# Query parts ahead of v in the first loads, half-width costs in the plan, and new orders, in a fused attention and MoE kernel

## The chip, the cores and the metric

The kernel runs on one core of a Trainium2 chip. The metric is the device time in microseconds (us) of one execution. A profiled execution gives one timeline for each engine: TensorE (PE, with its weight loads as PEld), VectorE (DVE), ScalarE (ACT), GpSimd (POOL), SyncE (SP) and the DMA queues.

## The reference

There are 8 batches of 8 heads, with 576 tokens of 64 values in q, k and v, and 32 packed queries p for each head. The attention has two steps: p attends to k and v, which gives 32 packed rows per head, and q attends to these packed rows. The result, 4608 tokens by 512, goes through two matrices with a smooth ReLU between them.

```python
p_packed = sm_attn(p, k, v)
out = sm_attn(q, p_packed, p_packed)
# x: out as 4608 tokens by 512
h = x @ w_in                       # 512 by 2048
g = np.where(h >= 1, h, np.where(h <= -1, 0, (h + 1) ** 2 / 4))
return g @ w_out                   # 2048 by 512
```

`sm_attn` is a softmax of the scores, scaled by 1/8, times the values. Outputs are float32.

## The kernel before, in words

**The work of one batch.** `attention(b, key)` loads k, q and v of a batch as bfloat16 with 96 partitions. PE transposes k (`by_array`, line 423, tiles `tp` to `kT`), forms the scores of p against k (`scores`, `sp`, line 459), ACT takes the exponential (`ex`), and PE multiplies by v (`packed`, `pk`, line 479, the row sums in line 485). Three small copies and an add give `ppT`, the packed rows. From batch 3 on, and for one part of batch 2, the transposes of q and k are made by DMA.

Instead of making the attention's output and then multiplying by w_in, the kernel multiplies the packed rows by w_in (`mk`, tiles `mp`, then cast to `M`, lines 649 to 668). The weights of the second softmax, `A`, are made in transposed form: scores `s`, exponential `eT`, sums over heads' rows `sm`, reciprocal as a logarithm `ln` and an exponential `rc`, and the product `A`. For batches from 1 on this is `weights`; for batch 0 it is `first_weights` (line 570), which treats the tokens in two halves, x = 0 and x = 1, and the heads in two groups, g = 0 and 1.

A hidden tile (`hidden_tile`, line 717) is one of 16 blocks of 128 hidden columns for a batch: four matmuls of `M` with `A` give `h` (line 733), and three operations apply the smooth ReLU: ACT evicts `h` to `x` (line 738), DVE or ACT does a second step (line 743 or 745), and DVE writes `hT` (line 748). An output tile (`out_tile`, line 778) is 128 tokens: 16 matmuls of `hT` with `w_out`, one for each hidden block fi = 0 to 15 in order, called an o step here (line 795). The tiles are counted for pairs of batches, nine for each pair; the first four of the first pair are cut in two by `CUTS`, with their first parts of 4, 4, 8 and 8 steps kept and added later.

**The order of the work.** `Plan` (line 60) is a list scheduler that runs while the program is built. Each task has an engine (or two to choose from), a cost from the table `C`, a key and its dependences. The plan follows a clock for each engine and takes the task that can start first; among those that start within `wait` times the best one's cost, the lowest key goes first. The order in which the plan takes tasks is the order of the instructions on each engine, and engines work their queues in that order. `slack` and `margin` are extra lags for PE behind the other engines. Where PE would wait at the start, the plan puts in dummy matmuls on zeros (line 870). `KEYS` holds keys for the tasks of each batch's attention, in the order of `FIRSTS` for batch 0 and `UNITS` for the others. A hidden tile's key is its batch plus fi/16, an output tile's is 100 or more, `p4` is the key of the transposes of p for batches 2 to 7, and `bk` less 1 that of the evictions of the first pair's output tiles.

**The loads.** All big loads are issued from POOL's queue, in one order: `FIRST` (line 38), then `ORDER` (line 23). `k0`, `k1`, `v0`, `v1` are the halves of batch 0's k and v by heads; `q00` and `q01` are the x = 0 tokens of q for the two groups of heads, `r` the x = 1 tokens. `i0` to `i4` are column blocks of w_in (256, 256, 512, 512 and 512 columns), `o0` to `o3` four parts of w_out, with four hidden blocks each; `k0`, `q1` and so on in `ORDER` belong to batch 1, and `p` is the rest of p. `IDENT` says before which of the first loads POOL makes the identity that the transposes use. `FLOW` and `C` hold the times that the plan gives each load.

**Splits.** `SPLIT` names blocks of `M` whose cast is made for each group of heads by itself; `HALVED` names the hidden tiles of batch 0 that are made for each half of the tokens; `MERGED` names the halves x for which `ln` and `rc` of batch 0 are made for both groups in one operation.

Of the kernel before, what the change touches and what calls it, by code (L numbers as in the profile page):

```python
# [11 lines left out]
C = dict(load=2.93, half=1.45, w_in=2.55, w_out=2.55, rest=1.25, out=3.2, p=4.3, land=1.13, xt=6.5, xland=9.0,  # L12
         tpp=0.06, tp=0.0425, sc=0.0295, pk=1.0, s2=0.245, sm=0.245, M=0.216, h=0.49, o=0.2158, switch=0.11,
         Tca=1.12, Tcd=0.75, ex=0.807, ppo=0.4, ppT=0.41, ppa=0.4, ppd=0.22, rs=0.165,
         eT=0.741, ln=0.651, rc=0.683, A=0.816, Mca=1.014, Mcd=1.223, x=0.651, ta=0.681, td=0.459, hT=0.757, oba=0.586, obd=0.69, hx=2.181,
         array=0.2, tell=0.04, lead=0.12, until=18.0, feed=0.2374, margin=0.3641, slack=0.1788, wake=1.2, warm=7.0, early=0.2216, wait=0.002722, p4=999.0, bk=115.3)
OVER = {"ACT": 0.104, "DVE": 0.083}
NW, NO, NX, NB = 3, 2, 5, 6
DW, FILL = 256, 512
CUTS = (4, 4, 8, 8)  # L20
PARTS = len(CUTS)

ORDER = 'r i0 i1 i4 o0 i2 q0 i3 k1 k0 o1 v q1 o2 o3 p'

FIRSTS = "kT0 kT1 sc0 sc1 pk0 pk1 q00 q01 q10 q11 s200 s201 s210 s211 sm00 sm01 sm10 sm11 M0 M1 M2 M3 M4".split()
UNITS = "kT0 kT1 qT0 qT1 sc0 sc1 pk0 pk1 s20 s21 sm0 sm1 M0 M1 M2 M3".split()
KEYS = [
# [8 lines left out]
SPLIT = ((0, 0), (0, 1), (0, 2))  # L36
LATE = ()
FIRST = "k0 k1 v0 v1 q00 q01"
IDENT = 3
FLOW = {"k0": 1.48, "k1": 1.52, "v0": 1.5, "v1": 1.46, "q00": 0.8, "q01": 0.8, "r": 1.6, "in0": 2.25, "in1": 1.33}  # L40
BLOCKS = {0: (0, 256, 512, 1024, 1536, 2048)}
HALVED = (0, 1, 2)
MERGED = (0, 1)

TURNED = 3
BY_DMA = {2: "q1"}
# [13 lines left out]
class Plan:  # L60
# [154 lines left out]
def kernel(  # L215
# [10 lines left out]
    nc = tc.nc  # L226
# [9 lines left out]
    P = 128  # L236
# [10 lines left out]
    X = 2  # L247
# [20 lines left out]
    PE, ACT, DVE, DMA, SP = "PE", "ACT", "DVE", "DMA", "SP"  # L268
    add = plan.add
# [33 lines left out]
    hT = hid.tile([P, KF, 2 * S], bf16)  # L303
# [109 lines left out]
    def attention(b, key):  # L413
# [6 lines left out]
        A = lambda: get(b, "A", lambda: att.tile([P, G, X, HALF], bf16, tag="A", name="A"))  # L420
# [149 lines left out]
        def first_weights(deps, r):  # L570
            tq, eTs, As = {}, {}, {}
            eT = lambda g: get(b, "eT" + str(g), lambda: att.tile([P, X, HALF], bf16, tag="eT", name="eT"))
# [35 lines left out]
            for x in range(X):  # L608
                boxes, own, cps = [{}, {}, {}], None, []
                for g in range(G):  # L610
                    t = add(PE, C["tp"] * 6, key["q%d%d" % (x, g)], [part_of["q", x, g]] + ([own] if g else []),
                            lambda x=x, g=g, bx=boxes[0]: turn(x, g, bx), takes=None if g else "W", readers=0 if g else 2, mode=1)
                    own = own or t
                    cps.append(both(lambda eng, x=x, g=g, bx=boxes[0]: copy(qT()[:, x, g * w:(g + 1) * w], bx["tp"][:, g, :w])(eng),
                                    C["Tca"] * 0.55, C["Tcd"] * 0.55, key["q%d%d" % (x, g)], [t], frees=own))
                    tq[x, g] = t
                own = None
                for g in range(G):
                    ky = key["s2%d%d" % (x, g)]
                    t = add(PE, C["s2"] / 2, ky, deps[g] + [cps[g]] + ([own] if g else []),  # L620
                            lambda x=x, g=g, bx=boxes[1]: inner(x, g, bx), takes=None if g else "W", readers=0 if g else 2, mode=2)
                    own = own or t
                    K.setdefault((b, "s2"), []).append(t)
                    eTs[x, g] = add(ACT, C["eT"] * 0.6, ky, [t, r[g]], lambda eng, x=x, g=g, bx=boxes[1]: nc.scalar.activation(
                        eT(g)[:, x], bx["s2"][:, g, :HALF], AF.Exp, scale=rs()[:, g, 1:]), frees=own)
                own, t2s, bx = None, [], boxes[2]
                merged = x in MERGED
                for g in range(G):
                    t = add(PE, C["sm"] / 2, key["sm%d%d" % (x, g)], [eTs[x, g]] + ([own] if g else []),
                            lambda x=x, g=g, bx=bx: sums(x, g, bx), takes=None if g else "W", readers=0 if g else (1 if merged else 2), mode=0)  # L630
                    own = own or t
                    t2s.append(t)
                part, prev = (1.0 if merged else 0.6), last.get("ln", [])
                made = []
                for gs in ([slice(G)] if merged else [slice(g, g + 1) for g in range(G)]):
                    ky = key["sm%d%d" % (x, gs.stop - 1)]
                    l_ = add(ACT, C["ln"] * part, ky, t2s[gs] + prev + made, lambda eng, gs=gs, bx=bx: ln(gs, bx), frees=own)
                    made = [add(ACT, C["rc"] * part, ky, [l_], lambda eng, gs=gs, bx=bx: inv(gs, bx))]
                    for g in range(G)[gs]:
                        As[x, g] = add(DVE, C["A"] * 0.56, key["sm%d%d" % (x, g)], made, lambda eng, x=x, g=g, bx=bx: nc.vector.scalar_tensor_tensor(  # L640
                            A()[:, g, x], eT(g)[:, x], rs()[:, g, :1], bx["rc"][:, g], ALU.mult, ALU.mult))
                last["ln"] = made
            K[b, "qt"] = list(tq.values())
# [5 lines left out]
        def mk(f, deps):  # L649
            box, ky, cs = {}, key["M" + str(f)], blocks(b)[f]  # L650
            n = cs.stop - cs.start

            def mm():
                mp = box["mp"] = wide([P, G, FW], f32, "mp")
                for a in range(Q):
                    for g in range(G):
                        h = head(g, a)
                        y = h % 2
                        nc.tensor.matmul(mp[a * NP:(a + 1) * NP, g, :n], pp_of(y, h),  # L659
                                         w_in_sb[y * D:(y + 1) * D, h // 2, cs], start=True, stop=True)  # L660

            gs = [slice(g, g + 1) for g in range(G)] if (b, f) in SPLIT else [slice(G)]
            need = [L["in", i] for i, c in enumerate(blocks(0)) if c.start < cs.stop and cs.start < c.stop]
            t, j = yield ky, C["M"] * n / FW, deps + need + K.get((b - 2, "h"), []), mm, len(gs)
            war = K.get((b - 2, "h"), [])
            part = {2: 0.56, 4: 1.0}[n // P] * (0.58 if len(gs) > 1 else 1.0)
            yield t, [both(lambda eng, g=g: copy(M()[:, g, cs], box["mp"][:, g, :n])(eng), C["Mca"] * part,
                           C["Mcd"] * part, ky, [t] + war, frees=(t, j)) for g in gs]

# [47 lines left out]
    def hidden_tile(b, fi, key, hs=None):  # L717
# [6 lines left out]
        box, col, hs = {}, (b % 2) * S, hs or list(range(X))  # L724
        n = len(hs)
        xs = slice(hs[0], hs[-1] + 1)
        pa, pd = (1.0, 1.0) if n == X else (0.6, 0.56)

        def mm():
            h = box["h"] = wide([P, X, FW], f32, "h")  # L730
# [22 lines left out]
        t_ = both(second, C["ta"] * pa, C["td"] * pd, key, [x_])  # L753
        lo = 0 if b % 2 == 0 else 4
        war = [step_of[b // 2 - 1, i, fi] for i in range(lo, lo + 5)] if b > 1 else []
        t_ = add(DVE, C["hT"] * pd, key, [t_] + war, third, frees=x_)
        for x in hs:
            wrote[b, fi, x] = t_
        return t
# [141 lines left out]
```

## Time and profile before

| | before |
|---|---|
| median of 3 runs | 248.5 us (247.53 to 248.61) |
| the profiled execution | 248.8 us |
| its span | 247.0 us |
| PE busy | 239.4 us (97%) |
| DVE busy | 175.3 us (71%) |
| ACT busy | 185.2 us (75%) |
| POOL busy | 31.3 us (13%) |
| mean granted clock of PE | 0.979 |

The span goes from the first to the last instruction; the remaining 1.8 us lie around it. A PE that is busy all the time isn't at its peak, since the ends of matmuls are modelled. In the rows of a timeline the columns are start, duration, engine and line, and in brackets the engine's idle time ahead of the entry and what ended it. An entry may hold several instructions (x12). Where the granted clock of a row is 0.50, matmuls run at half speed.

### The profile page before, as it was taken

How to read it: one execution, taken by the hardware profiler on the slowest of the kernel's cores; microseconds unless marked ns; L12 is line 12 of the kernel's file. 1: busy time of each engine (PE TensorE's matmuls, PEld its weight loads, DVE VectorE, ACT ScalarE, POOL GpSimd, SP SyncE). 2: the span in 40 equal slices, each digit the busy share in tenths (PEclk: the TensorE clock that was granted, in tenths of full speed). 3: DMA queues.
4: the chain of work that ended last, by engine and by line, in shares of the span. 5: the costliest groups of instructions: out<-in, count | busy, mean ns of one | idle time of the engine just before them, and what ended most of it. 6: DMA issues, size and time to landing. Idle time of an engine off the chain costs nothing.

```text
span 247.0 us, 5472 instructions
## 1 busy us (share of the span) xinstructions
PE 239.4 (97%) x2221; PEld 138.0 (56%) x2221; DVE 175.3 (71%) x314; ACT 185.2 (75%) x310; POOL 31.3 (13%) x46
## 2 busy tenths in 40 slices
PE   7689999999999999999999999999999999999994
PEld 2544567467644666357745664576545674476443
DVE  5336999689964699339987995389752997589400
ACT  3328998889967796769998997699466995899410
POOL 8652431210110102002101110000000000000000
PEclk9956999999999999999999999999999999999999
DMA  7999999999999999999999999634433102210232
GB/s 105 170 201 205 204 204 202 198 232 201 192 196 185 204 130 168 180 168 203 181 166 147 197 155 178 137 74 84 90 93 85 42 3 73 57 44 3 60 110 86
DMA packets 57258, 34.67 MB, mean 140 GB/s; under 512 B 30224, under 2 KB 52752, under 8 KB 57232
## 3 DMA queue, kind: packets, MB, share of 16 engines
q0 software_dynamic: 25984, 18.55, 53.2%
q1 hardware_dynamic: 31104, 15.70, 35.1%
q8 instruction: 17, 0.28, 0.5%
q10 hardware_dynamic: 144, 0.07, 0.1%
q14 instruction: 9, 0.07, 0.1%
HBM read 37.22 MB, written 9.44 MB: 189 GB/s over the span
## 4 chain that ended last, share of the span: by engine, by line
PE 93%; DMA 3%; POOL 1%; issue 1%; DVE 1%; ACT 0%; POOLq 0%
PE o L795 51%; PE h L733 26%; PE mp L659 4%; DMA v<-in_v_dram 3%; PE pk L479 2%; PE sp L459 2%; PE tp L432 1%; PE sm L528 1%; PE o L870 1%; PE s L513 1%; PE pk L485 1%; PE tp L582 1%; PE s L591 1%; PE sm L597 0%; POOL k L293 0%
## 5 line engine op out<-in xcount | busy, mean ns | idle before, releaser
L795 PE MATMUL o<-w_out_sb,hT 128*128 128x512 bf16 (+2 forms) x592 | 143.7, 374 | 0.0
L748 DVE SCALAR_TENSOR_TENSOR hT<-x 128x576 bf16<-128x576 f32 (+1 forms) x131 | 90.4, 737 | 0.6
L795 PEld LDWEIGHTS <-hT 128*128 128x128 bf16 x592 | 54.9, 98 | 53.9 <-issue 5.3
L738 ACT ACTIVATE x<-h 128x576 f32<-128x576 f32 (+1 forms) x131 | 76.5, 653 | 7.0 <-PE h L733 6.7
L733 PE MATMUL h<-A,M 128*128 128x288 bf16 x512 | 75.4, 287 | 0.0
L733 PEld LDWEIGHTS <-M 128*128 128x128 bf16 x512 | 49.9, 98 | 22.6 <-issue 1.3
L743 DVE TENSOR_SCALAR x<-x 128x576 f32<-128x576 f32 (+1 forms) x75 | 31.8, 450 | 9.8 <-ACT x L738 9.7
L745 ACT ACTIVATE x<-x 128x576 f32<-128x576 f32 (+1 forms) x56 | 37.5, 697 | 0.1
L375 DVE CAST M<-mp 128x1024 bf16<-128x1024 f32 (+1 forms) x16 | 17.9, 1122 | 13.3 <-PE mp L659 11.0
L375 ACT COPY ob<-o 128x512 f32<-128x512 f32 (+1 forms) x19 | 10.9, 575 | 20.7 <-PE o L795 20.2
L375 DVE COPY ob<-o 128x512 f32<-128x512 f32 (+1 forms) x14 | 9.5, 679 | 20.4 <-PE o L795 20.3
L375 ACT CAST M<-mp 128x1024 bf16<-128x1024 f32 (+2 forms) x20 | 17.6, 912 | 6.8 <-PE mp L659 6.5
L462 ACT ACTIVATE ex<-sp 96x768 bf16<-96x768 f32 x16 | 13.0, 815 | 4.0 <-PE sp L459 4.0
L548 DVE SCALAR_TENSOR_TENSOR A<-eT,rs,rc 128x576 bf16<-128x576 bf16 x12 | 9.8, 816 | 8.0 <-ACT rc L538 8.0
L293 POOL DMA_DIRECT2D k<-in_k_dram x10 | 7.6, 764 | 49.9 <-DMA kT<-k 36.8
L523 ACT ACTIVATE eT<-s,rs 128x576 bf16<-128x576 f32 x14 | 9.8, 746 | 2.7 <-PE s L513 2.4
L293 POOL DMA_DIRECT2D q<-in_q_dram x8 | 6.2, 777 | 42.6 <-DMA qT<-q 21.7
L533 ACT ACTIVATE ln<-sm 128x576 f32<-128x576 f32 x14 | 9.1, 652 | 3.1 <-PE sm L528 2.9
L870 PE MATMUL o<-zeros 128*128 128x512 bf16 (+1 forms) x25 | 10.2, 503 | 1.2 <-DVE zeros L281 1.2
L659 PE MATMUL mp<-w_in_sb,ppT 64*32 64x512 bf16 (+1 forms) x264 | 10.8, 380 | 0.0
L538 ACT ACTIVATE rc<-ln 128x576 f32<-128x576 f32 x14 | 9.6, 682 | 0.4
L459 PEld LDWEIGHTS <-kT 128*128 128x128 bf16 x192 | 7.8, 98 | 2.5 <-DVE kT L375 0.2
(61 smaller groups left out, 129.5 us busy)
## 6 DMA issues: line engine op xcount, KB each, us to landing
out_dram<-ob SPq DMA_DIRECT2D x23, 192.0 KB, 2.9
v<-in_v_dram POOLq DMA_DIRECT2D x7, 576.0 KB, 15.6
k<-in_k_dram POOLq DMA_DIRECT2D x6, 576.0 KB, 16.4
q<-in_q_dram POOLq DMA_DIRECT2D x6, 576.0 KB, 12.1
out_dram<-ob SPq DMA_DIRECT2D x22, 128.0 KB, 3.6
w_out_sb<-in_moe_w_out_dram POOLq DMA_DIRECT2D x4, 512.0 KB, 16.9
w_in_sb<-in_moe_w_in_dram POOLq DMA_DIRECT2D x3, 512.0 KB, 13.2
out_dram<-ob SPq DMA_DIRECT2D x22, 64.0 KB, 2.4
```

The source lines that it names most:

```text
L293: nc.gpsimd.dma_start(tok[nm, b][:, hs].rearrange("p h c d -> p h (c d)"), SRC[nm][b, hs].rearrange("h (p c) d -> p h (c d)", c=NC))
L375: return lambda eng: nc.vector.tensor_copy(out_, in_) if eng == DVE else nc.scalar.copy(out_, in_)
L459: nc.tensor.matmul(o[:, :, a], kT()[:, i, w:w + P], pT[:, b, h], start=True, stop=True)
L462: nc.scalar.activation(ex()[:, :, i].rearrange("p e x a n -> p e (x a n)"), box["sp"], AF.Exp, scale=scale)
L659: nc.tensor.matmul(mp[a * NP:(a + 1) * NP, g, :n], pp_of(y, h), w_in_sb[y * D:(y + 1) * D, h // 2, cs], start=True, stop=True)
L733: nc.tensor.matmul(h[:, hf, :HALF], T[b, "M"][:, g, fi * P:(fi + 1) * P], T[b, "A"][:, g, hf], start=(g == 0), stop=(g == G - 1))
L738: nc.scalar.activation(box["x"], box["h"][:, xs, :HALF], AF.Prelu, bias=-1.0, alpha=0.5)
L743: nc.vector.tensor_scalar(x, x, 1.0, 0.0, ALU.add, ALU.max)
L745: nc.scalar.activation(x, x, AF.Relu, bias=1.0)
L748: nc.vector.scalar_tensor_tensor(hT[:, fi, col + xs.start * HALF:col + xs.stop * HALF].rearrange("p (a t) -> p a t", a=n), box["x"], 1.0, ...
L795: nc.tensor.matmul(box["o", j, part][:, :cs.stop - cs.start], hT[:, fi, i * P:(i + 1) * P], w_out_sb[:, fi, cs], start=(fi == 0 or fi in c ...
L870: plan.run(lambda w: nc.tensor.matmul(o[:, :w], zeros[:, :P], zeros[:, :w], start=True, stop=True))
```

## The change

The first loads are issued as k0 k1 q00 q01 v0 v1 instead of k0 k1 v0 v1 q00 q01. In `ORDER` w_in's block 2 goes ahead of block 4, batch 1's k goes earlier and its q later, and p ahead of the last two parts of w_out. No cast of `M` is split any more, hidden tile 3 of batch 0 is halved as well, and no `ln` and `rc` are merged. In the plan the costs of half-width operations change, as do the lags, the wait and the keys; the key of p's transposes falls from 999 to 52.94, and that of the first pair's evictions from 114.3 to 0.07. All eight rows of `KEYS` are new (cut here).

```diff
-         array=0.2, tell=0.04, lead=0.12, until=18.0, feed=0.2374, margin=0.3641, slack=0.1788, wake=1.2, warm=7.0, early=0.2216, wait=0.002722, p4=999.0, bk=115.3)
+         array=0.2, tell=0.04, lead=0.12, until=18.0, feed=0.2686, margin=0.4074, slack=0.492, wake=1.2, warm=7.0, early=0.247, wait=0.1491, p4=52.94, bk=1.07)
...
-ORDER = 'r i0 i1 i4 o0 i2 q0 i3 k1 k0 o1 v q1 o2 o3 p'
+ORDER = 'r i0 i1 i2 o0 i4 k0 i3 k1 o1 v q1 q0 p o2 o3'
...
-SPLIT = ((0, 0), (0, 1), (0, 2))
+SPLIT = ()
...
-FIRST = "k0 k1 v0 v1 q00 q01"
+FIRST = "k0 k1 q00 q01 v0 v1"
...
-FLOW = {"k0": 1.48, "k1": 1.52, "v0": 1.5, "v1": 1.46, "q00": 0.8, "q01": 0.8, "r": 1.6, "in0": 2.25, "in1": 1.33}
+FLOW = {"k0": 1.48, "k1": 1.52, "q00": 0.8, "q01": 0.8, "v0": 1.5, "v1": 1.46, "r": 1.56, "in0": 1.5, "in1": 2.0}
...
-HALVED = (0, 1, 2)
-MERGED = (0, 1)
+HALVED = (0, 1, 2, 3)
+MERGED = ()
...
-                                    C["Tca"] * 0.55, C["Tcd"] * 0.55, key["q%d%d" % (x, g)], [t], frees=own))
+                                    C["Tca"] * 0.6, C["Tcd"] * 0.6, key["q%d%d" % (x, g)], [t], frees=own))
...
-                    eTs[x, g] = add(ACT, C["eT"] * 0.6, ky, [t, r[g]], ...
+                    eTs[x, g] = add(ACT, C["eT"] * 0.675, ky, [t, r[g]], ...
...
-                        As[x, g] = add(DVE, C["A"] * 0.56, key["sm%d%d" % (x, g)], made, ...
+                        As[x, g] = add(DVE, C["A"] * 0.63, key["sm%d%d" % (x, g)], made, ...
...
-            part = {2: 0.56, 4: 1.0}[n // P] * (0.58 if len(gs) > 1 else 1.0)
+            part = {2: 0.57, 4: 1.0}[n // P] * (0.63 if len(gs) > 1 else 1.0)
...
-        pa, pd = (1.0, 1.0) if n == X else (0.6, 0.56)
+        pa, pd = (1.0, 1.0) if n == X else (0.63, 0.62)
...
-        t_ = add(DVE, C["hT"] * pd, key, [t_] + war, third, frees=x_)
+        t_ = add(DVE, C["hT"] * (1.0 if n == X else 0.59), key, [t_] + war, third, frees=x_)
```

The constant `hx`, by which the key of a halved tile's second half is raised, falls from 2.181 to 0.06524.

More of the change, by code (lines that the diff above doesn't have):

```diff
@@ L14 @@
          Tca=1.12, Tcd=0.75, ex=0.807, ppo=0.4, ppT=0.41, ppa=0.4, ppd=0.22, rs=0.165,
-         eT=0.741, ln=0.651, rc=0.683, A=0.816, Mca=1.014, Mcd=1.223, x=0.651, ta=0.681, td=0.459, hT=0.757, oba=0.586, obd=0.69, hx=2.181,
-         array=0.2, tell=0.04, lead=0.12, until=18.0, feed=0.2374, margin=0.3641, slack=0.1788, wake=1.2, warm=7.0, early=0.2216, wait=0.002722, p4=999.0, bk=115.3)
+         eT=0.741, ln=0.651, rc=0.683, A=0.816, Mca=1.014, Mcd=1.223, x=0.651, ta=0.681, td=0.459, hT=0.757, oba=0.586, obd=0.69, hx=0.06524,
+         array=0.2, tell=0.04, lead=0.12, until=18.0, feed=0.2686, margin=0.4074, slack=0.492, wake=1.2, warm=7.0, early=0.247, wait=0.1491, p4=52.94, bk=1.07)
 OVER = {"ACT": 0.104, "DVE": 0.083}
@@ L623, in first_weights @@
                     K.setdefault((b, "s2"), []).append(t)
-                    eTs[x, g] = add(ACT, C["eT"] * 0.6, ky, [t, r[g]], lambda eng, x=x, g=g, bx=boxes[1]: nc.scalar.activation(
+                    eTs[x, g] = add(ACT, C["eT"] * 0.675, ky, [t, r[g]], lambda eng, x=x, g=g, bx=boxes[1]: nc.scalar.activation(
                         eT(g)[:, x], bx["s2"][:, g, :HALF], AF.Exp, scale=rs()[:, g, 1:]), frees=own)
@@ L639, in first_weights @@
                     for g in range(G)[gs]:
-                        As[x, g] = add(DVE, C["A"] * 0.56, key["sm%d%d" % (x, g)], made, lambda eng, x=x, g=g, bx=bx: nc.vector.scalar_tensor_tensor(
+                        As[x, g] = add(DVE, C["A"] * 0.63, key["sm%d%d" % (x, g)], made, lambda eng, x=x, g=g, bx=bx: nc.vector.scalar_tensor_tensor(
                             A()[:, g, x], eT(g)[:, x], rs()[:, g, :1], bx["rc"][:, g], ALU.mult, ALU.mult))
```

16 rows, old and new, of the table KEYS are left out of this document.

## The prediction

> **What bounds the kernel now.** I read the page first, for the busiest engine and the chain that ended last.
>
> ```profile
> span 247.0 us, 5472 instructions
> ...
> PE 239.4 (97%) x2221; PEld 138.0 (56%) x2221; DVE 175.3 (71%) x314; ACT 185.2 (75%) x310; POOL 31.3 (13%) x46
> ...
> PE 93%; DMA 3%; POOL 1%; issue 1%; DVE 1%; ACT 0%; POOLq 0%
> PE o L795 51%; PE h L733 26%; PE mp L659 4%; DMA v<-in_v_dram 3%; PE pk L479 2%; PE sp L459 2%; PE tp L432 1%; PE sm L528 1%; PE o L870 1%; PE s L513 1%; PE pk L485 1%; PE tp L582 1%; PE s L591 1%; PE sm L597 0%; POOL k L293 0%
> ```
>
> TensorE (PE) carries 93% of the chain. The change takes no matmul of the result away and adds none, so time can only come from PE time that is not such work. The second view is the sums by stage, to see where PE stops being held up (columns: PE, weight loads, DVE, ACT, POOL, granted clock, DMA share, GB/s).
>
> ```profile
> 17.20:20.00 2.80, 2.60 (x23) 0.91 (x22) 0.82 (x2) 2.02 (x4) 0.75 (x1) 0.50 1.24 206
> 20.00:26.00 6.00, 6.00 (x42) 2.83 (x41) 5.56 (x14) 4.98 (x13) 2.25 (x3) 0.74 1.26 205
> 26.00:40.00 14.00, 14.00 (x146) 9.07 (x145) 13.76 (x26) 13.34 (x25) 5.04 (x6) 1.00 1.28 205
> ```
>
> From 26 to 40 us PE is full, and DVE (13.76 of 14 us) and ACT (13.34) nearly so. From 17.2 to 20 us DVE works 0.82 us and ACT 2.02 of 2.8. PE looks nearly full (2.60) there too, but at half clock (0.50) and in part with the dummy matmuls on zeros that the plan puts into waits. So the kernel has a head of some 20 us that is a chain of waits, then a stretch where all three compute engines are full, then PE alone. A microsecond won in the head moves everything behind it, unless a load arrives too late for the earlier clock time.
>
> The head is read from PE's weight loads, which show when each first load landed: an entry starts right behind the transfer in its bracket.
>
> ```profile
> 9.99 0.41 PEld L479 LDWEIGHTS <-v 96*128 96x128 bf16 x12 [0.92 <-DMA v<-in_v_dram]
> ...
> 11.47 0.41 PEld L479 LDWEIGHTS <-v 96*128 96x128 bf16 x12 [0.89 <-DMA v<-in_v_dram]
> ...
> 12.24 0.31 PEld L582 LDWEIGHTS <-q 96*64 96x64 bf16 x12 [0.21 <-DMA q<-in_q_dram]
> ...
> 13.02 0.13 PEld L582 LDWEIGHTS <-q 96*64 96x64 bf16 x1 [0.31 <-DMA q<-in_q_dram]
> ```
>
> v0 is usable at 9.99, v1 at 11.47, q00 at 12.24, q01 at 13.02. What follows v1 and q01 is read from the chain of waits.
>
> ```profile
> 12.84 0.32 DVE ppT L375
> ...
> 13.19 0.47 DVE qT L375
> ...
> 13.70 0.69 PE tp L582 x12
> 14.39 0.39 PE s L591 x4
> ```
>
> The packed p for v1 is done at 13.16 (12.84 and 0.32), 1.69 us after v1. But the product s starts only at 14.39: 1.2 us go into q01's transposes and a copy of qT, done after q landed. The chain then reaches the normalised A like this, ACT first, then DVE, then the first h on PE:
>
> ```profile
> 14.80 0.50 ACT L624 ACTIVATE eT<-s,rs 128x288 bf16<-128x288 f32 x1 [2.38 <-PE s L591]
> 15.83 0.50 ACT L624 ACTIVATE eT<-s,rs 128x288 bf16<-128x288 f32 x1 [0.53 <-PE s L591]
> 17.63 0.65 ACT L602 ACTIVATE ln<-sm 128x576 f32<-128x576 f32 x1 [1.30 <-PE sm L597]
> 18.64 0.89 ACT L624 ACTIVATE eT<-s,rs 128x288 bf16<-128x288 f32 x2 [0.35 <-PE s L591]
> 19.42 0.68 ACT L607 ACTIVATE rc<-ln 128x576 f32<-128x576 f32 x1
> ```
> ```profile
> 20.41 0.43 DVE L375 CAST M<-mp 128x256 bf16<-128x256 f32 x1 [2.31 <-ACT M L375]
> 20.75 0.94 DVE L640 SCALAR_TENSOR_TENSOR A<-eT,rs,rc 128x288 bf16<-128x288 bf16 x2
> 21.61 0.42 DVE L375 CAST M<-mp 128x256 bf16<-128x256 f32 x1
> 21.94 0.94 DVE L640 SCALAR_TENSOR_TENSOR A<-eT,rs,rc 128x288 bf16<-128x288 bf16 x2
> ```
> ```profile
> 21.41 0.96 PE L733 MATMUL h<-A,M 128*128 128x288 bf16 x3
> ```
>
> Three waits here are order, not work. The first ln waits 1.30 us for the sums of both groups, as it is merged. The rc of the first half of the tokens (x0) waits for two eT of the second half (x1). The A of x0 waits for the cast of M, which was scheduled late.
>
> **The change part by part.** *Loads.* q00 and q01 move ahead of v. The bytes up to the last of the four are the same, so v1 is usable at about 13.02, where q01 was: 1.55 us later. v0, one v part of 1.48 us (9.99 to 11.47) earlier, comes at about 11.5. q01 comes one v pair earlier, at about 9.5. Its transposes and copies then lie where PE and DVE wait for v: hidden. If that cover were gone, they cost the 1.2 us again. On POOL three loads stand ahead of the identity in both orders, so nothing else is delayed there. The later loads up to the first w_in part land as before, since the same bytes stand in front:
>
> ```profile
> 14.80 0.68 POOL L293 DMA_DIRECT2D k<-in_k_dram  x1 [0.79 <-DMA q<-in_q_dram]
> 16.13 0.68 POOL L293 DMA_DIRECT2D k<-in_k_dram  x1 [0.65 <-DMA w_in_sb<-in_moe_w_in_dram]
> 17.85 0.75 POOL L326 DMA_DIRECT2D w_out_sb<-in_moe_w_out_dram  x1 [1.04 <-DMA w_in_sb<-in_moe_w_in_dram]
> 20.04 0.79 POOL L293 DMA_DIRECT2D v<-in_v_dram  x1 [1.44 <-DMA w_in_sb<-in_moe_w_in_dram]
> ```
>
> POOL's waits for landings put r (the x1 queries) before 14.80 and the w_in parts before 16.13, 17.85 and 20.04. The third part is now block 2 (columns 512 to 1024) instead of block 4, which feeds the hidden tiles 4 to 7 that the o steps need first.
>
> A rule of the Trainium skill speaks against this part: DMA: Bandwidth & Descriptors, Specifications, asks for at least 512 B per transfer for line rate. A row of the first q parts has 3 x 64 bf16 values, 384 B, and one of v 768 B. By the trace q01 came 0.78 us after q00, for half the bytes of a v part that took 1.48: the same rate within 6%. So the trace does not bear the rule out. By the rule, if the extra read is taken as half rate (an estimate), v1 would come 1.5 us later still, x0's gain below would be 1.9 instead of 3.4, and the sum some 0.4 us poorer.
>
> *The chain behind v1 (x0).* 13.02 and the 1.69 us to ppT give 14.71. r is there at about the same time and one group of its transposes may stand first, up to the 0.69 us of 13.70; half of it, 0.35, gives s at 15.06. In the trace eT (14.80) starts 0.41 us behind its s (14.39), so eT runs from 15.47 to 15.97. For the sums, also short matmuls ahead of an ACT operation, I take 0.41 again: ln at 16.4. ln and rc are no longer merged: each is half wide. No half-wide ln is in the trace; the bounds are the two half-wide ACT operations, x at 413 ns (below) and eT at 500; I take 0.45, near to x, as both write f32. ln and rc then end at 17.3. One A takes 0.47 (half of 0.94): A is done at 17.8, and with 0.2 for hand-overs h starts at about 18.0 instead of 21.41: 3.4 us earlier. M0 is not late: its w_in part is there before 16.13, and matmul and cast take about 1 us.
>
> *x1.* r lands as before, so eT of x1, which ended at 19.53, gains only what stood ahead of it in the orders; I take 0.8, the length of its own pair, hence 18.7. Behind it stand four half-wide ln and rc (1.8 us) and two half-wide x evictions (0.8) on ACT, to 21.3, then one A: 21.7 instead of 22.88, 1.2 us earlier.
>
> *Work added and removed on ACT and DVE.*
>
> ```profile
> L748 DVE SCALAR_TENSOR_TENSOR hT<-x 128x576 bf16<-128x576 f32 x125 | 88.0, 751 | 0.5
> ...
> L738 ACT ACTIVATE x<-h 128x576 f32<-128x576 f32 x125 | 74.3, 665 | 6.6 <-PE h L733 6.2
> ...
> L748 DVE SCALAR_TENSOR_TENSOR hT<-x 128x288 bf16<-128x288 f32 x6 | 2.5, 447 | 0.0
> ...
> L738 ACT ACTIVATE x<-h 128x288 f32<-128x288 f32 x6 | 2.3, 413 | 0.5 <-PE h L733 0.5
> ...
> L375 ACT CAST M<-mp 128x512 bf16<-128x512 f32 x2 | 1.1, 618 | 0.0
> ```
>
> Unmerging: 8 operations of 0.45 for 2 of 0.65 and 2 of 0.68: +0.94. Halving hidden tile 3: +0.16 on ACT (2 x 0.413 less 0.665), +0.14 on DVE (2 x 0.447 less 0.751), and about +0.15 for the operation between: +0.45. Undoing the split of M0 and M1: two casts of 0.42 become one of 0.62, twice: -0.44; M2's two of 0.62 for a whole one are taken as equal. Sum +0.95 us over two engines that are full from then on: 0.5 us of time.
>
> *What comes out of it.* In the 8.8 us from 17.2 to 26 DVE works 0.82 + 5.56 = 6.38 us and ACT 2.02 + 4.98 = 7.0: 2.42 and 1.8 idle. Were both full from 17.2 on, that is 4.22 us over two engines, 2.1 us of time, less the 0.5: 1.6 us. PE by itself would allow between 1.2 (x1's gain) and 3.4 (x0's). I take 2.0: near to 1.6, since these two engines are what is full next, and a little above it, since the earlier block 2 gives the o steps their inputs sooner.
>
> *Later loads and orders.* p now goes ahead of w_out parts 2 and 3, which land later by its time.
>
> ```profile
> 20.00:41.60 21.60, 7.10 (x24) 2.08 (x24) 0.93 1.27 205
> 41.60:44.40 2.80, 1.84 (x7) 0.55 (x7) 1.00 1.72 182
> ```
> ```profile
> 26.60 0.75 POOL L326 DMA_DIRECT2D w_out_sb<-in_moe_w_out_dram  x1 [0.69 <-DMA q<-in_q_dram]
> 29.16 1.19 POOL L331 DMA_DIRECT2D p_nat<-in_p_dram  x1 [1.81 <-DMA w_in_sb<-in_moe_w_in_dram]
> ```
> ```profile
> DMA to landing us min/median/max: 17.7/17.7/17.7
> ```
> ```profile
> p_nat<-in_p_dram POOLq DMA_DIRECT2D x1, 192.0 KB, 16.6
> ```
>
> Part 3, issued at 26.60, landed 17.7 us later, at 44.3; p, behind it, at 45.8: 1.5 us of transfer. The first 24 o steps (to 41.6 us) use parts 0 and 1 alone; steps 29 to 32 of tile 0 use part 2 and 33 to 36 part 3. So by 44.4, when 31 steps are done, part 3 is wanted as it lands. With PE 2.0 us ahead and the part 1.5 later, work must be found elsewhere for 3.5 us: tile 1's steps 4 to 7 (4 x 0.217 us, the rate shown below, is 0.9), the transposes of p, which come earlier, and batch 1's products. I take 0.4 us lost; bounds 0 and 3.5.
>
> *Steady orders.* From 26 us on PE shows no idle time (14.00 of 14), but its busy time can hide stalls. The chain has a stretch of o steps alone:
>
> ```profile
> 203.68 4.55 PE o L795 x21
> ```
>
> That is 0.217 us a step. All 592, of which the last tile's 32 come to 16 whole ones, are 576 x 0.217 = 125 us, against 51% of 247.0, 126: about 1 us of stalls to win, and I bound the other side by as much. The plan's lags for PE grow (slack, margin), which takes stalls away: -0.2.
>
> Sum: -2.0 + 0.4 - 0.2 = -1.8 us on the profiled 248.8 (span 247.0 and 1.8 around it): 247.0. The median of the three runs is 248.5, 0.3 below the profiled run, so the forecast is 246.7.
>
> **The rivals.** *The late w_out parts decide (slower).* Place: the o steps 29 to 36, at 40 to 46 us. If PE has nothing to run there, 3.5 us are lost against 2.0 won; with half of the steady bound, +0.5, that is +2.0: 250.5. It decides once more than 2.0 of the 3.5 us stay empty. For: the steps up to 44.4 are taken as parts land. Against: at 26 to 40 us ACT and DVE held PE's inputs back, so batch 1's work is there to fill. Between the two lies a draw: about 2.0 of the 3.5 lost, 248.5.
>
> *x0's path decides alone.* If the two full engines can let x1 wait while x0's tiles feed PE, 3.4 us come, with the steady bound of -1.0 and nothing lost to loads 4.4: 244.1. For: PE still has room for it, as its chain runs dummies (line 870) even here:
>
> ```profile
> 20.28 0.85 PE o L870 x2
> ```
>
> Against: the 1.6 us of ACT and DVE.
>
> *The clock.* The granted clock is 0.50 from 17.2 to 20 and 0.74 over 20 to 26. If the transposes keep PE at work in the wait for v and the clock stays up, the cold 0.69 us transposes and the sums shorten; an estimate is 0.5 us more gain, 246.2, inside the range. The Trainium skill, TensorE: Matmul & The Clock Gate, Part 4, says that transposes don't count as busy for the clock; by it there is no such gain, and my sum takes none.
>
> **How the numbers follow.** Forecast, with the clock's variant: 0.47. x0 alone: 0.12. The draw: 0.23. Slower: 0.18. The three runs spread from 247.53 to 248.61, so about 0.5%, 1.24 us, is what can be told from no change. The forecast's -1.8 lies just beyond it; with x0's case that makes faster 0.57, within 0.26 (the draw and the forecast's weak edge), slower 0.17. The range, 244.2 to 250.0, reaches from x0's case nearly to the slow one and leaves about 1 in 10 out on each side; the likeliest case by itself (a gain of 0.9 to 3.1) spans 245.4 to 247.6.
>
> **What would show it.** Right: q's transposes (line 582) between 8 and 11 us; the second packed p near 14.7; half-wide ln and rc; the first h near 18.0; no DVE gap of 2.3 us before 20; PE full of results from about 23 to 24. Wrong: the first h after 20.5 (then x0's chain did not shorten); v1's product well after 13.5; o steps waiting for w_out between 41 and 46; PE busy below full after 50.

## The result, and the profile after

| | before | changed |
|---|---|---|
| median of 18 runs each, side by side | 248.69 us (247.53 to 249.43) | 246.17 us (245.26 to 248.59) |
| the profiled execution | 248.8 us | 246.91 us |
| its span | 247.0 us | 245.1 us |
| mean granted clock of PE in it | 0.979 | 0.986 |

The ratio is 0.9914, with an interval of 0.9893 to 0.9935: by it the changed kernel is 2.1 us (0.9%) faster. The profiled executions differ by 1.9 us; the sum of the prediction was 1.8.

The page of the changed kernel, with the lines that answer to those shown of before, and the row of the granted clock in 40 slices of 6.1 us:

```profile
span 245.1 us, 5442 instructions
...
PE 234.3 (96%) x2186; PEld 139.1 (57%) x2223; DVE 175.0 (71%) x311; ACT 185.5 (76%) x317; POOL 31.8 (13%) x46
...
PEclk9689999999999999999999999999999999999999
...
PE 72%; DVE 16%; ACT 6%; issue 3%; DMA 2%; POOL 0%; ACTq 0%; POOLq 0%
```

Some matmul records are missing here (2186 against 2223 weight loads), so the lower sum of PE is no sign of less work. Below, o steps are counted by their weight loads: 592 in both kernels. The share of PE in the chain fell from 93% to 72%. Where PE, ACT and DVE are nearly full together, the chain can pass through any of them, and gaps left by missing records send it there too; where the time went is therefore read from the stages:

```profile
17.20:20.00 2.80, 1.35 (x26) 0.62 (x26) 2.10 (x5) 2.27 (x8) 1.02 (x2) 1.00 1.24 206
20.00:26.00 6.00, 5.98 (x53) 3.67 (x46) 5.25 (x14) 5.94 (x17) 2.22 (x3) 1.00 1.26 206
26.00:40.00 14.00, 13.68 (x172) 9.38 (x175) 13.92 (x27) 13.08 (x23) 5.47 (x7) 1.00 1.39 200
```

DVE now works 2.10 of the 2.8 us from 17.2 to 20 (0.82 before), and the clock is whole there (0.50 before). The head, on PE:

```profile
9.14 0.69 PE L582 MATMUL tp<-ident,q 96*64 96x96 bf16 x12
9.77 0.82 PE L459 MATMUL sp<-pT,kT 128*128 128x64 bf16 x12
10.52 0.69 PE L582 MATMUL tp<-ident,q 96*64 96x96 bf16 x12
11.54 0.63 PE L870 MATMUL o<-zeros 128*128 128x512 bf16 x1 [0.33 <-issue]
11.97 0.85 PE L479 MATMUL pk<-ex,v 96*128 96x64 bf16 x12
12.63 0.33 PE L485 MATMUL pk<-ones,ex 96*128 96x2 bf16 x6
12.81 1.23 PE L870 MATMUL o<-zeros 128*128 128x512 bf16 x3
13.83 0.72 PE L479 MATMUL pk<-ex,v 96*128 96x64 bf16 x12
...
15.64 0.30 PE L591 MATMUL s<-qT,ppT 64*32 64x288 bf16 x4
...
18.62 0.28 PE L597 MATMUL sm<-eT,onesblk 128*128 128x288 bf16 x1 [0.49 <-ACT eT L624]
19.64 0.28 PE L597 MATMUL sm<-eT,onesblk 128*128 128x288 bf16 x1 [0.74 <-ACT ln L602]
19.86 0.30 PE L659 MATMUL mp<-w_in_sb,ppT 64*32 64x256 bf16 x8
20.09 0.42 PE L733 MATMUL h<-A,M 128*128 128x288 bf16 x2
```

The transposes of q (line 582) lie between 9.14 and 11.2, ahead of v's products, as forecast. v0 landed at 11.43 and v1 at 12.94 (forecast 11.5 and 13.02). But the product with v1 starts only at 13.83: three dummies on zeros stand before it and take 0.4 us each, as the clock is at half from 7.43 to 14.26. The first h comes at 20.09 instead of 21.41.

### The profile page after: what moved, and what is told of

Its sections match the earlier page's. It is cut to its first block, busy times and chain, and to the rows that moved or that the text cites. A ratio compares the mean times of both kernels' runs of the same rounds, so it can differ in the third digit from the quotient of the medians.

```text
span 245.1 us, 5442 instructions
## 1 busy us (share of the span) xinstructions
PE 234.3 (96%) x2186; PEld 139.1 (57%) x2223; DVE 175.0 (71%) x311; ACT 185.5 (76%) x317; POOL 31.8 (13%) x46
## 4 chain that ended last, share of the span: by engine, by line
PE 72%; DVE 16%; ACT 6%; issue 3%; DMA 2%; POOL 0%; ACTq 0%; POOLq 0%
PE o L795 42%; PE h L733 16%; DVE hT L748 10%; DVE x L743 3%; ACT x L738 3%; PE mp L659 2%; PE sp L459 2%; PE pk L479 2%; DMA k<-in_k_dram 2%; PE tp L432 2%; PE sm L528 1%; ACT x L745 1%; PE s L513 1%; PE pk L485 1%; PE tp L582 1%
## 5 line engine op out<-in xcount | busy, mean ns | idle before, releaser
L795 PE MATMUL o<-w_out_sb,hT 128*128 128x512 bf16 (+2 forms) x557 | 135.8, 373 | 1.9 <-issue 0.5
L733 PE MATMUL h<-A,M 128*128 128x288 bf16 x512 | 74.6, 286 | 0.6 <-issue 0.2
L745 ACT ACTIVATE x<-x 128x576 f32<-128x576 f32 (+1 forms) x59 | 39.0, 691 | 0.1
L743 DVE TENSOR_SCALAR x<-x 128x576 f32<-128x576 f32 (+1 forms) x73 | 30.9, 453 | 11.0 <-ACT x L738 11.0
L375 ACT COPY ob<-o 128x512 f32<-128x512 f32 (+1 forms) x22 | 12.7, 578 | 17.5 <-PE o L795 17.3
L375 DVE CAST M<-mp 128x1024 bf16<-128x1024 f32 (+1 forms) x16 | 18.9, 1188 | 8.3 <-PE mp L659 8.2
L375 ACT CAST M<-mp 128x1024 bf16<-128x1024 f32 (+1 forms) x17 | 16.3, 992 | 5.5 <-PE mp L659 5.5
L375 DVE COPY ob<-o 128x512 f32<-128x512 f32 (+1 forms) x11 | 7.4, 676 | 15.5 <-PE o L795 15.4
L293 POOL DMA_DIRECT2D v<-in_v_dram x9 | 6.7, 751 | 23.9 <-PE pk L485 21.2
L870 PE MATMUL o<-zeros 128*128 128x512 bf16 (+1 forms) x25 | 8.4, 446 | 1.5 <-DVE zeros L281 1.2
```

Of the source, the lines that this page charges most:

```text
L293: nc.gpsimd.dma_start(tok[nm, b][:, hs].rearrange("p h c d -> p h (c d)"), SRC[nm][b, hs].rearrange("h (p c) d -> p h (c d)", c=NC))
L375: return lambda eng: nc.vector.tensor_copy(out_, in_) if eng == DVE else nc.scalar.copy(out_, in_)
L733: nc.tensor.matmul(h[:, hf, :HALF], T[b, "M"][:, g, fi * P:(fi + 1) * P], T[b, "A"][:, g, hf], start=(g == 0), stop=(g == G - 1))
L743: nc.vector.tensor_scalar(x, x, 1.0, 0.0, ALU.add, ALU.max)
L745: nc.scalar.activation(x, x, AF.Relu, bias=1.0)
L795: nc.tensor.matmul(box["o", j, part][:, :cs.stop - cs.start], hT[:, fi, i * P:(i + 1) * P], w_out_sb[:, fi, cs], start=(fi == 0 or fi in c ...
```

## The experiments

The theory (A): q's transposes are off the path behind v1, which is what was forecast, and the plan must have set the engines' orders for it. Rival B: the transposes and dummies in the wait for v only keep the clock up, and that is the gain. Rival C: the unmerged `ln` and `rc`, the new order of the later loads or the new keys bring it. The expectations below use the same letters, each as its own text defines them. Each ratio is to the kernel before, run on the same chip; the intervals are of 95%.

### The load order alone, with the plan remade

On the kernel before:

```diff
-FIRST = "k0 k1 v0 v1 q00 q01"
+FIRST = "k0 k1 q00 q01 v0 v1"
```

> The kernel before with one line changed: the first loads in the new order (q00 and q01 ahead of v); the plan makes its orders anew from the old keys and costs. Theory A (q's transposes leave the chain behind v1, which itself lands 1.5 us later): -1.2 us for the transposes and the copy, +1.5 for v on the first group's path, so between -1.0 and +0.5, 247.7 to 249.2. Rival B (the load order is what frees the head, orders are secondary): the whole gain, near 246.2. Rival C (only the new orders and costs gain): +1.0 to +1.5, near 250.

Measured: 246.17 us against 247.99, ratio 0.9932 (0.9903 to 0.9962). The one line, with the old costs, keys, merges and later loads, brings what the whole change brings. That is the time of this run's B; its A, which counted v's later landing against the gain, missed it (247.7 to 249.2). PE in the head:

```profile
10.84 0.52 PE L479 MATMUL pk<-ex,v 96*128 96x64 bf16 x12 [0.38 <-DMA v<-in_v_dram]
...
12.31 0.52 PE L479 MATMUL pk<-ex,v 96*128 96x64 bf16 x12 [0.25 <-DMA v<-in_v_dram]
...
13.92 0.30 PE L591 MATMUL s<-qT,ppT 64*32 64x288 bf16 x4
...
18.42 0.83 PE L733 MATMUL h<-A,M 128*128 128x288 bf16 x3
```

Here the products of v wait for v alone, nothing stands between them and s but the copies (and dummies in the wait for them), and the first h comes at 18.42, 3.0 us earlier than before, with `ln` and `rc` still merged. The lead stays: the last o step comes at 240.45, against 243.59 before. Rival C is not needed. But the clock was whole in this trace and not in that of before, so B is still open. As far as the clock that a run lists can be trusted (see below), the runs that list 0.998 or more speak against B as the whole gain: 12 of this kernel have a median of 246.17, 8 of before one of 247.05.

### The order of issue alone, with the old orders on the engines

On the kernel before; the plan still reckons with v first:

```diff
-        for n, nm in enumerate(FIRST.split()):
+        for n, nm in enumerate("k0 k1 q00 q01 v0 v1".split()):
```

> The kernel before, its plan and the orders on all engines unchanged; only the issue of the first loads on POOL's queue is in the new order (q00 and q01 ahead of v). Theory A (the gain is q's transposes and copies moved off the chain behind v1, which takes the plan): PE still takes v's products first, v lands 1.5 us later and the chain behind it keeps its length, less the 0.3 us that PE waited for q01: 0.5 to 1.5 us slower than before, 249 to 250. Rival (the load order acts by itself, through the DMAs): as the version with the plan made anew, 246.2 to 246.8.

Measured: 249.76 us against 248.0, ratio 1.0079 (1.0053 to 1.0104): slower by 2.0 us by the ratio, a little more than the 0.5 to 1.5 that A expected here, at a listed clock of 0.970 to 0.979. PE in the head:

```profile
12.27 0.52 PE L479 MATMUL pk<-ex,v 96*128 96x64 bf16 x12 [0.53 <-DMA v<-in_v_dram]
12.63 0.29 PE L485 MATMUL pk<-ones,ex 96*128 96x2 bf16 x6
12.85 0.69 PE L582 MATMUL tp<-ident,q 96*64 96x96 bf16 x12
14.37 0.69 PE L582 MATMUL tp<-ident,q 96*64 96x96 bf16 x12 [0.82 <-DVE qT L375]
14.99 0.43 PE L591 MATMUL s<-qT,ppT 64*32 64x288 bf16 x4
...
22.08 1.15 PE L733 MATMUL h<-A,M 128*128 128x288 bf16 x4
```

q lands ahead of v here, but its transposes still stand behind v's products, at 12.85 and 14.37; v comes later, and everything with it. The earlier landing of q is worth nothing by itself. What gains is the new landing together with orders made for it. In the head the place of 24 transposes in PE's order is what is seen to differ; it was not changed by itself, apart from the other orders.

### Without dummies in the head

The same edit on three kernels: before, changed, and before with the load order alone. It leaves out the dummies that the plan would put in after 9 us:

```diff
-            if self.count["O"] < 3:
+            if self.count["O"] < 3 and self.now["PE"] < 9.0:
```

> The kernel before without the dummy matmuls after 9 us of the plan's clock. Theory A (its head waits for loads and orders, the dummies fill only waits): 248.7, within 0.5. Rival B (the clock decides): the half clock lasts beyond 23 us and costs 1 us or more, 249.7 and above.

> The changed kernel without the dummy matmuls after 9 us of the plan's clock. Theory A (the head is a chain; the dummies ahead of v0's and v1's products run at half clock past the landing of v and hold v1's product up by 0.7 to 0.9 us): 0.5 to 1.0 us faster, 245.3, even if the clock stays low longer. Rival B (the clock decides: without dummies it stays at half to 20 us and more): 1 to 2 us slower, 247.2 to 248.2.

> The kernel before with the first loads in the new order, the plan made anew and no dummy matmuls after 9 us of its clock; beside the old order without dummies (248.6 at a mean clock of 0.972, 1.0036 of before). Theory A (the chain is shorter, whatever the clock does): 1.2 to 2.0 us less at the same clock, 246.6 to 247.4. Rival B (the early q transposes only keep PE at work, so that the clock stays up; the chain gains nothing): equal at the same clock, 248.6.

| kernel | with dummies | without |
|---|---|---|
| before | 1 | 1.0036 (1.0008 to 1.0063) |
| changed | 0.9914 (0.9893 to 0.9935) | 0.9973 (0.9947 to 0.9999) |
| load order alone | 0.9932 (0.9903 to 0.9962) | 0.9992 (0.9975 to 1.0008) |

All three lose without dummies: 0.4% to 0.6%, 0.9 to 1.5 us (0.3% for the changed kernel against its second measurement below, 0.9946). For before A was right (248.7 expected, 248.6 measured). For the changed kernel it expected a gain of 0.5 to 1.0 us and missed; the time, 247.26, lies where B put it. Without dummies the load order alone is 0.44% ahead of before (0.9992 against 1.0036), 1.1 us of the 1.7 that it brings with them. The two intervals together leave 0.3 to 1.9 us for it (an estimate), so the gain isn't the clock alone; but the 0.6 us that would be left for the dummies and the clock can't be told from nothing.

The two traces without dummies show less than the medians: the 24th o step at 39.20 with the load order alone and at 39.35 in before. That trace of before is one of its faster runs (247.93, median 248.6), and its first loads landed earlier: v1 at 10.26, against 11.43 in the trace with dummies, in the same load order. Such a difference is as large as the gain that is looked for, so one trace against one trace doesn't decide it.

### The changed kernel once more, and with more dummies

> The changed kernel unchanged, for more runs beside the next ones. In the runs so far the time goes with the granted clock: 245.47 where it never fell, 247.2 where the mean was 0.986. Theory B (the clock in the head is the largest part of a run's distance from the best): again near 245.5 at a mean clock of 1.00 and 247.2 at 0.986, and in a profile at full clock the first h near 18.0 to 18.5. Theory A alone (orders decide): no such link.

Measured, unchanged: 247.01 us against 248.38, ratio 0.9946 (0.9921 to 0.9971). Its profiled run had the clock whole until 19.0 us, and the head of that run comes nearer to the one that the prediction describes:

```profile
11.13 0.52 PE L479 MATMUL pk<-ex,v 96*128 96x64 bf16 x12 [0.60 <-DMA v<-in_v_dram]
...
12.59 0.52 PE L479 MATMUL pk<-ex,v 96*128 96x64 bf16 x12 [0.25 <-DMA v<-in_v_dram]
...
14.20 0.30 PE L591 MATMUL s<-qT,ppT 64*32 64x288 bf16 x4
...
18.66 0.42 PE L733 MATMUL h<-A,M 128*128 128x288 bf16 x2
```

With the same instructions in the same order, h comes 1.4 us earlier than in the first profile. So the clock in the head differs from run to run. The 1.4 us don't last: the clock is at half from 19.0 to 22.4 us here, the first o step comes at 24.76 (24.66 in the first profile), the last at 241.80 (241.68), and the span is 245.3 us against 245.1. An earlier first h is thus no measure of the end by itself. Of the 18 runs of the changed kernel 7 list a mean clock of 1.00, with a median of 245.47 us, and 5 list 0.986, with one of 247.2. The kernel before lists 0.998 to 1.00 in 8 of 35 runs (247.05) and 0.979 in 17 (248.42). In the 12 new runs of the changed kernel the link is weaker than expected: four list 1.00, with a median of 246.1 (245.51 to 246.8), and four 0.986, with one of 247.0 (246.64 to 247.84). The load order alone lists 0.998 or more in all its 12 runs, and they still spread from 245.66 to 248.12. So the listed clock goes with a part of the spread and doesn't account for all of it; time before the first record of the clock counts as 1.00 in it.

A kernel with more dummies from 4.5 to 9.2 us:

```diff
+            if e == "PE" and fill and 4.5 < at < 9.2:
+                fill += FILL
```

> The changed kernel with two more dummy matmuls of 512 columns, one for each of two of the waits between the transposes of p and the products of v (5 to 9 us). Theory B (the clock falls because PE is idle between 5 and 7.4 us): the mean clock is 0.998 or more in nearly all runs and the time is 245.5. Rival (the dummies stand in front of k's work and cost what they win, or the clock falls in any case): 246.2 or more, clocks spread as before.

Measured: 246.74 us, ratio 0.993 (0.9901 to 0.9958). Three of 8 runs list a whole clock and five 0.993, none 0.986; B expected a whole clock in nearly all and 245.5 us, and missed. Against the unchanged kernel on the same chip (0.9946) the intervals overlap: inconclusive.

### p behind w_out again

On the changed kernel:

```diff
-ORDER = 'r i0 i1 i2 o0 i4 k0 i3 k1 o1 v q1 q0 p o2 o3'
+ORDER = 'r i0 i1 i2 o0 i4 k0 i3 k1 o1 v q1 q0 o2 o3 p'
```

> The changed kernel with the load of p put back behind the last two parts of w_out, as before. Theory A (o steps 29 to 36 wait for the late parts; from 40 to 46 us the changed kernel gives back about 0.7 us of its lead): 0.5 to 1.0 us faster than the changed kernel, about 245.4. Rival (other work fills that stretch, and the parts are not waited for): as the changed kernel, 246.2, or slower by the later transposes of p.

Measured: 246.85 us against 247.99, ratio 0.9948 (0.9917 to 0.9979). No gain over the changed kernel: the rival was right, and A missed. The o steps alone (line 795; the counts of weight loads are the second ones), of the changed kernel and then of this one:

```profile
20.00:41.60 21.60, 7.06 (x25) 2.43 (x30) 1.00 1.34 202
41.60:44.40 2.80, 1.43 (x5) 0.33 (x6) 1.00 1.25 205
44.40:50.00 5.60, 4.25 (x18) 1.76 (x18) 1.00 1.32 204
```
```profile
20.00:41.60 21.60, 8.06 (x29) 2.40 (x30) 0.95 1.27 205
41.60:44.40 2.80, 1.82 (x7) 0.47 (x7) 1.00 1.78 182
44.40:50.00 5.60, 4.51 (x19) 1.58 (x17) 1.00 1.32 204
```

In both, 30 steps are done by 41.6 us (24 before) and 54 by 50.0. In the changed kernel the last w_out parts landed at 42.44 and 45.11, and no o step waited for one. So the late parts cost nothing.

### The merges back in

On the changed kernel, alone and then with the last output issued by SP instead of ACT:

```diff
-MERGED = ()
+MERGED = (0, 1)
...
-                (nc.scalar if j else nc.sync).dma_start(dst[:, cs], ob[a:a + n])
+                nc.sync.dma_start(dst[:, cs], ob[a:a + n])
```

> The changed kernel with ln and rc of batch 0 merged again for both groups. Theory A (half-wide ln lets the first group start early; x0's path is what counts): 0.3 to 0.8 us slower, 246.5 to 247. Rival (ACT is full behind it, and merging saves 0.9 us of its work): equal or up to 0.4 us faster.

> The changed kernel with ln and rc merged, as in the run that took 249.2, and with the very last output piece issued from SP's queue instead of ACT's. In that run's trace the last o step started at 241.6, as in the changed kernel, but ACT's last issue took 2.30 us instead of 0.37, with an 8 KB instruction fetch at 243.06 inside it. Theory (the fetch of ACT's instructions falls into the last issue, and merging has no cost of its own): about 247.0, 1.9 to 2.2 us faster than that run. Rival (merging costs in the head): 248.5 to 249.2.

Measured, the merges alone: 249.18 us against 248.38, ratio 1.0026 (1.0001 to 1.0051), slower than both theories allowed. That looks like a price for the waits of merged operations. It is at most a part of it: the last o step comes at 241.6 us in its trace, as in the changed kernel. The difference is on ACT at the very end. The changed kernel, then the merged one:

```profile
242.03 0.27 ACT L375 COPY ob<-o 128x128 f32<-128x128 f32 x1 [2.95 <-PE o L795]
242.33 0.37 ACTq L810 DMA_DIRECT2D out_dram<-ob  x1
```
```profile
241.97 0.27 ACT L375 COPY ob<-o 128x128 f32<-128x128 f32 x1 [2.95 <-PE o L795]
242.27 2.30 ACTq L810 DMA_DIRECT2D out_dram<-ob  x1
```

The same issue takes 2.30 us instead of 0.37. In the trace an 8 KB transfer of the queue of kind "instruction" lies inside it, at 243.06; in the changed kernel that transfer lies at 232.9, in mid-stream. With the last issue on SP the merged kernel took 247.06 us, ratio 0.9974 (0.9950 to 0.9998), the time that was expected; by the ratios that is 1.3 us less than with the issue on ACT. Its trace holds such an 8 KB transfer in the last microseconds too, but ACT has nothing to issue there. So most of the slowness came from where ACT's long issue fell, not from the merges; ACT runs 313 instructions instead of 317, which by inference moves that place. In the traces of before, of the load order alone and of both runs of the changed kernel the last issue takes 0.37 us, so the main result doesn't come from there. Whether merging costs anything in the head, at most some 0.7 us by the ratio of the unchanged kernel (0.9946), can't be told from these runs.

### The keys

The changed kernel with the old table of keys whole, and the kernel before with the new load order and rows 1 to 7 of the new table (here the first of these rows; in the other kernel the rows go the other way):

```diff
-    [-2.689, -1.805, -0.374, -0.207, -0.209, -2.362, -1.727, 0.056, -1.812, -1.880, -2.943, -1.728, -2.666, -0.208, -2.111, -0.422],
...
+    [0.256, -2.259, -3.274, -2.771, -0.603, -2.679, -0.895, -0.602, -0.604, -2.704, -2.221, -2.440, -3.048, -2.402, -2.257, 1.582],
...
```

> The changed kernel with the old table of keys; all else is as changed. Theory C (the new orders carry a gain of their own beside the loads): 0.5 to 1.5 us slower than the changed kernel, 246.7 to 247.7. Rival (the loads and what the plan makes of them carry it): within 0.4 us of the changed kernel at the same clock.

> The kernel before with the first loads in the new order and the new rows of keys for batches 1 to 7; the row for batch 0, the costs, the splits and the later loads stay old. The old keys in the changed kernel lost about 0.8 us after 100 us of the span. Theory C (the new rows carry a gain of their own): 0.5 to 1.0 us faster than the load order alone, about 245.4, which would beat both kernels. Rival (the rows fit only the costs and lags that they were made for): 246.2 or more.

Measured: 247.68 us, ratio 0.9975 (0.9951 to 0.9999), and 249.52 us against 248.0, ratio 1.0069 (1.0044 to 1.0093). The second is a clear miss for the theory that the new rows are better by themselves; the rival stated with it was right. From 60 to 80 us, all engines, with the old keys and the load order alone, and then with the new rows:

```profile
60.00:80.00 20.00, 20.00 (x206) 10.86 (x205) 12.48 (x20) 14.79 (x24) 1.54 (x2) 1.00 1.28 203
```
```profile
60.00:80.00 20.00, 18.68 (x202) 10.33 (x204) 10.89 (x19) 13.09 (x20) 2.32 (x3) 1.00 1.28 193
```

PE is full in the first and stands still for 1.3 us in the second (two of its 204 matmuls there have no record). From the 24th to the last o step the new rows take 207.1 us, the old ones 203.4. So the new rows under the old costs, loads and first row took away all of the 1.7 us and more: that is shown. The old table under the new costs took some 0.7 us more than the changed kernel (0.9975 against 0.9946), but the intervals overlap, and that side isn't shown.

## Why the prediction was right, point by point

**The loads.** Right within 0.1 us for v in the first profile: v0 at 11.43 and v1 at 12.94. POOL's waits for the two end 0.3 us behind:

```profile
11.72 0.68 POOL L293 DMA_DIRECT2D k<-in_k_dram  x1 [1.26 <-DMA v<-in_v_dram]
13.22 0.74 POOL L324 DMA_DIRECT2D w_in_sb<-in_moe_w_in_dram  x1 [0.82 <-DMA v<-in_v_dram]
```

q01 landed at 8.98; my 9.5 doesn't follow from its terms, as 13.02 less a v pair of 2.96 is 10.1. The closeness is partly luck, since landings move from run to run: v1 landed at 12.54 in the second profile and at 12.26 in the load order alone, and the 11.43 of before, on which the forecast rests, is 10.26 in the trace of that kernel without dummies.

**The chain behind v1.** Right in its mechanism, shown from both sides: the load order with the plan gains (0.9932), the load order without it loses (1.0079). Its size was off, and two errors cancel in part: in the second profile, with the clock whole up to there, s comes at 14.20 (taken: 15.06) and h at 18.66 (18.0). From s to h the forecast takes 2.9 us; both profiles show 4.45. In the first profile h comes at 20.09, between "right" and the 20.5 at which the step was to be called wrong, and v1's product at 13.83 is past the 13.5 given there. Three things were not in the sum. Dummies at half clock in front of v's products cost 0.9 us between v1's landing at 12.94 and 13.83 (in the second profile, at whole clock, the product starts at 12.59, just behind the landing). PE's order puts a `sm` of x1, which waits 0.74 us for ACT, and an `mp` in front of h, which therefore starts 0.6 us after the last A of x0 is done at 19.45. And ACT's order is not the one I assumed:

```profile
16.39 0.40 ACT L602 ACTIVATE ln<-sm 128x288 f32<-128x288 f32 x1
16.83 0.44 ACT L607 ACTIVATE rc<-ln 128x288 f32<-128x288 f32 x1
17.18 0.40 ACT L602 ACTIVATE ln<-sm 128x288 f32<-128x288 f32 x1
18.07 0.50 ACT L624 ACTIVATE eT<-s,rs 128x288 bf16<-128x288 f32 x1 [0.50 <-PE s L591]
18.47 0.43 ACT L607 ACTIVATE rc<-ln 128x288 f32<-128x288 f32 x1
```

The second `rc` of x0 stands behind an eT of x1, which waits 0.50 us for its product: one group of x0 ends at 17.3, the other at 18.9, and h needs both. My chain followed the operations of one group. The half-wide duration itself, 0.45 by estimate, is 0.40 for `ln` and 0.43 to 0.44 for `rc`.

**Work added (0.5 us).** Its effect is not to be seen: with `ln` and `rc` merged or not, the last o step is at 241.6 us, though the clock in the heads of those traces differs, and the load order alone reaches 246.17 with the merges on.

**The head's gain (2.0 us).** The 24th o step is 1.5 us ahead of before (38.74 against 40.22), the 100th 2.0 (71.37 against 73.38), the last 1.9 (241.68 against 243.59). So the head gave 1.5 us, 1.4 in the second profile, and what follows gave 0.4 more: from the 24th to the last o step 202.9 and 203.0 us in its two profiles, against 203.4 in before and in the load order alone. The forecast had 2.0 won and a net 0.2 lost. Its sum of 1.8 is near because the two are off in opposite directions, which is luck. That ACT and DVE set the 1.6 isn't shown: the load order alone, at whole clock, leads by 3.1 us at its 24th step (37.09), with x1's A done at 20.31 where the changed kernel has 22.43 and 21.05.

**The later loads (0.4 us lost).** This step failed: nothing is lost to the late parts. At the 48th step only 0.8 us of the lead are left (48.37 against 49.18), which looks like it, but with p behind w_out the 48th comes at 48.34 as well. What stands there is work moved ahead. The transposes of p, in the changed kernel and then in before:

```profile
44.94 0.86 PE L389 MATMUL tpp<-ident,p_nat 128*64 128x128 bf16 x24
```
```profile
49.70 0.86 PE L389 MATMUL tpp<-ident,p_nat 128*64 128x128 bf16 x24
```

They lie ahead of the 48th step in the one and behind it in the other: 0.86 us that are not lost. They are not the only work that changed places, as the lead is down to 0.8 at the 31st step already (42.43 against 43.25), ahead of them; but it is 2.0 again at the 100th. The rival of the late w_out parts, and the draw that hung on it, fell.

**x1.** Its A is done at 22.43 in the first profile and 21.05 in the second (taken: 21.7; before: 22.88). The rival that x0 decides alone, with 3.4 us or more, fell: h came 2.8 us earlier than before in the second profile, and the lead further on was 1.4 to 1.9.

**The steady orders (-0.2 us).** The 0.4 us behind the 24th step bear out the direction; what in the new orders gives them wasn't tried. In the whole time they don't show: load order alone 0.9932, the whole change 0.9914 and 0.9946.

**The clock.** I gave it 0.5 us and no weight in the sum. Between runs of one kernel more than that goes with it: 245.47 against 247.2 us in the first runs of the changed kernel, 246.1 against 247.0 in the later ones. The pairs without dummies leave open how much of the gain goes with it. The forecast of 246.7 may owe a part of its nearness to two omissions of opposite sign that lie in one median: dummies at half clock ahead of v's products, and runs at whole clock. The Trainium skill, TensorE: Matmul & The Clock Gate, Part 4, says that transposes don't count as busy for the clock. The runs don't settle it: the mean was 0.998 to 1.00 in all 12 runs of the load order alone, and fell in 11 of 18 runs of the changed kernel, with the same transposes in the wait for v.

**Open:** what lets the clock fall at 7.4 us in one run, at 19.0 in another and, in the trace of the load order alone, not before the end; and why the same loads land up to 1.2 us earlier in one run than in another. The changed kernel with the old load order alone and a plan made for it wasn't tried.

## What to carry to other kernels

A load that is moved ahead may gain only if the engines' orders are set for it: here the same loads gave 0.7% with the orders remade and cost 0.8% without. New keys can take away a gain when the costs and loads that they were found with stay behind (here 0.9932 became 1.0069), so an edit and its keys are judged together. A sum can be right with its terms off, so each term is held against the trace: here 1.5 and 0.4 us won, not 2.0 won and 0.2 lost. Before a slower or faster run is put down to the edit, look at the granted clock of each run, at the last output's issue and at when the first loads landed: the first two went with 0.9 to 1.7 and 1.9 us here, against the change's 2.1, and the same loads landed up to 1.2 us apart.

## What the runs showed of the hardware

- A DMA issue on ACT took 2.30 us instead of 0.37 where an 8 KB instruction transfer lay inside it. It was the kernel's last issue, and the span was 1.9 us longer with the last o step at the same place (241.6 us). That ACT stood still for its own instructions is inferred from the two lying together in one trace; that the time fell with the issue on SP, from 1.0026 to 0.9974 of before, is measured.
- The clock fell and rose in whole steps of about 3.41 us: half from 12.9 to 23.2 us in before (three steps), 7.43 to 14.26 in the changed kernel (two), 19.0 to 22.4 in its second profile (one), 12.2 to 25.9 in before without dummies (four). By the Trainium skill, TensorE: Matmul & The Clock Gate, Part 1, the window is 3413 ns and runs freely, so that the same kernel meets it at different phases; the steps agree with the length, and the spread between runs of one kernel with the phase.
- The clock's row shows full speed up to its first record even where PE is slow: in the load order alone without dummies the mean is listed as 1.0, yet v's products of 12 take 0.82 us there against 0.52 with dummies.
- The same first loads in the same order landed at different times: v1 at 11.43 us in before and at 10.26 in before without dummies, with k1 at 7.33 in both; with q first, v1 at 12.94 and 12.54 in the two profiles of the changed kernel and at 12.26 in the load order alone. No run shows why.
